# M_prev's products on quarters of TensorE's array, attention ordered anew, and a second quarter of weights split early

## The chip, the core and the metric

The kernel runs on one NeuronCore of a Trainium2 chip. The core has five engines, each with its own queue that it works through in order: PE (TensorE, the matmuls; PEld is its weight load), DVE (VectorE), ACT (ScalarE), POOL (GpSimd) and SP (SyncE, which here only issues transfers). The metric is the device time of one execution in microseconds (us). Before the change the median of 3 runs is 961.65 us (960.67 to 963.48).

## The reference

Three stages follow each other. Each one's output is the next one's input.

```python
# attention, with B, H, S, D = 4, 8, 576, 64
scores = q @ k.T / sqrt(D), causal;  a = softmax(scores);  local = a @ v
q_p = where(q > 0, q, exp(q) - 1) + 1
mem_out = (q_p @ M_prev) / (q_p @ z_prev + 1e-6)
x = g * mem_out + (1 - g) * local          # g = sigmoid(beta), one number per head
# mixture of experts: 2304 tokens, 8 experts, 512 -> 1024 -> 512
logits = x @ w_gate;  e = argmax(logits);  p = softmax(logits)[e]
x = p * (relu(x @ w1[e]) @ w2[e])
# last network: 512 -> 2048 -> 512
out = elu(x @ w_in) @ w_out
```

All arrays are float32.

## The kernel before, in words

Attention works on 16 pairs of heads (`pair(p)`), four pairs to a batch. For one pair, in the names of the code: q and k are loaded and transposed on PE (L568); `parts` makes a high and a low part of each in `ab` (L582 or L585, then L589); `phi_in` and the two steps behind it make q_p in `qpT`, the exponential and the positive part on ACT (L602 to L610), the rest on POOL (L626, L627); `scores` makes five blocks of query rows (L665 and L669 for blocks 0 to 3, L676 and L677 for block 4), DVE takes each block's extreme (L685), ACT the exponential `a` (L690); `weights` transposes `a` on PE (L703) and ACT or DVE copies it out to `aA` and `aB` (L515, L518); L804 multiplies with v, giving `xT`. Two products on quarters of the array follow (helper `quarters`, L527): `mb` with `qpT` for the memory, and `iw` with `xT` for the logits. DVE scales them into `ms` and `ls` (L781 to L789, L824) and POOL adds them up (L836). All of these products share four PSUM buffers of two banks (`pat`).

Ahead of the first pair, `constants` loads M_prev into `mb`, transposes its 32 matrices on PE (L340), copies them out (L344) and multiplies each with `w_gate` (L353), so that `mb` holds M_prev, M_prev times w_gate, and z_prev (L354). Matmuls without a use (`keep_busy`, L249) run meanwhile.

After every fourth pair `gate_plan` finds each token's expert and rank on DVE and PE (L871 to L950), after the third batch `routing` decides what the first four tiles of 128 tokens are, SP loads the first tile's weights (L1167), and POOL gathers the first tile's rows (L1181, into the buffer `ex` that `phi_in` used last). `first_parts` splits these rows (L1192) and the first of the eight quarters of the tile's weights (L1209 or L1206 for the high part, L1212 for the low) while attention still runs. The second stage, `moe`, then takes the tiles (L1335 and L1378 are its products, three for each in high and low parts), and at the same time widens the last network's weights through the buffers `wide` (class `Widen`); `moe2` is the last stage.

What sets the order: every step is an `Op` of a planner (`Plan`) with its engines, a cost number, what it reads and writes, and a priority. `order` simulates the engines with the cost numbers, picks at each step the ready operation with the lowest priority number on an engine that is free, and the program is emitted in that order, engine by engine. Of two engines it takes the one that would end first. `stick` keeps PE in one shape of the array as long as something of that shape is ready. The priorities' offsets are the table `KNOBS`. Nothing is reordered on the chip: an engine waits for the instruction at the head of its queue.

Of the kernel before, what the change touches and what calls it, by code (L numbers as in the profile page):

```python
# [24 lines left out]
NI = 5  # L25
# [58 lines left out]
class Plan:  # L84
# [52 lines left out]
    def order(self):  # L137
# [7 lines left out]
        while len(done) < len(self.ops):  # L145
# [43 lines left out]
            if e == "PE":  # L189

                n = int(t / self.TICK)
                cold = work.get(n - 1, self.warm if n == 0 else 0.0) < self.DUTY * self.TICK
                end = t + o.cost * (1.0 + cold) + (self.wait if o.waits else 0.0) + (self.DRAIN if o.mode != mode else 0.0)
                mode = o.mode
                for m in range(n, int(end / self.TICK) + 1):
                    part = min(end, (m + 1) * self.TICK) - max(t, m * self.TICK)
                    work[m] = work.get(m, 0.0) + o.dense * o.cost * part / max(1.0, end - t)
# [56 lines left out]
def constants(tc, ctx, c, M_prev, z_prev, beta, w_gate):  # L254
# [78 lines left out]
    for h in range(2):  # L333
        for n in range(2):
            def mk(h, n):
                bk = Slot(c.rs)

                def f():
                    for x in range(8):
                        nc.tensor.transpose(bk.t[0:D, x * D:(x + 1) * D], c.mb[hss[h], 8 * n + x, 0:D], c.ident[hss[h], hss[h]])  # L340
                pl.op("PE", 450, f, r=["mld"], w=[bk], prio=K["mem"] - 30)

                def f():
                    nc.scalar.copy(mT[:, h, 8 * n:8 * n + 8, :].rearrange("p x d -> p (x d)"), bk.t[0:D, 0:512])  # L344
                pl.op("ACT", ca(512), f, r=[bk], w=[("mT", h, n)], prio=K["mem"] - 30)
            mk(h, n)
    for h in range(2):
        def mk(h):
            bq = Slot(c.rs)

            def f():
                for x in range(NPAIR):
                    nc.tensor.matmul(bq.t[hss[h], x * E:(x + 1) * E], mT[:, h, x, :], wg[:, 2 * (x % (H // 2)) + h, :], start=True, stop=True)  # L353
                nc.tensor.matmul(bq.t[hss[h], 256:256 + B * H], zr, c.ident[0:B * H, 0:B * H], start=True, stop=True)  # L354
            pl.op("PE", 900, f, r=["mld", ("mT", h, 0), ("mT", h, 1), ("raw", 0, 0), ("raw", 0, 1)], w=[bq], prio=K["mem"] - 20, dense=0.15)

            def f():
                nc.vector.tensor_copy(c.mb[hss[h], :, D:XB], bq.t[hss[h], 0:NPAIR * E].rearrange("p (x e) -> p x e", e=E))
                nc.vector.tensor_copy(c.mb[hss[h], :, XB:MW].rearrange("p x o -> p (x o)"),
                                      bq.t[hss[h], 256:256 + B * H].rearrange("p (x h) -> p x h", h=2)[:, :, h])  # L360
            pl.op("DVE", 400, f, r=[bq], w=["mb"], prio=K["mem"] - 20)
        mk(h)
# [100 lines left out]
def cps(n):  # L463
    return 330 + 0.83 * n


def cpt(n):
    return 150 + 2.1 * n


def attention(tc, ctx, c, q, k, v, M_prev):
# [19 lines left out]
    r_q, r_k = padded("q", K["nq"], [P, NI, 2, D], lambda t: t[0:D, NI - 1]), padded("k", K["nq"], [P, NI, 2, D], lambda t: t[D:P, NI - 1])  # L491
# [369 lines left out]
def gate_plan(tc, c, b, lg, xrow, rl, rx, ring, pr):  # L861
# [4 lines left out]
    def bc(x):  # L866
# [4 lines left out]
        (330, lambda: v.tensor_reduce(G.L, lg.t.rearrange("p i c e -> p i e c"), axis=AX.X, op=ALU.add)),  # L871
# [772 lines left out]
def kernel(ctx, tc, q, k, v, M_prev, z_prev, beta, w_gate, w1, w2, w_in, w_out, out):  # L1644
# [41 lines left out]
    with ExitStack() as s1:  # L1686
# [3 lines left out]
        c.wq = [[ep.tile([P, 1024], F32R, name=f"wq{n}{i}") for i in range(2)] for n in range(1)]  # L1690
# [82 lines left out]
```

## Time and profile before

| | |
|---|---|
| median of 3 runs | 961.65 us |
| the profiled execution | 961.42 us, of which the span from the first to the last instruction is 959.7 us |
| attention, to the first product of the first tile | 0 to 245.5 us |
| mixture of experts, to the last network's first product | 245.5 to about 553 us |
| last network | about 553 us to the end |
| PE busy | 930.1 us, 97% of the span |
| DVE, ACT, POOL busy | 639.3, 447.4, 181.5 us |

The profile records one execution. A row of a timeline gives the start, the duration from the first instruction of the row to the end of its last, the engine, the code's line, output and inputs, and how many instructions were merged; in brackets stands how long the engine sat idle before, and what ended it. A float32 product that isn't a transpose shows as two records. PEclk is the clock that TensorE was granted, 1.00 for 2.4 GHz and 0.50 for 1.2 GHz; a stretch in which it changes shows a value between.

### The profile page before, as it was taken

The page shows a single profiled execution, that of the slowest core. Times are in us where ns is not written, and L with a number is a line of the kernel's source. Part 1 is how long each engine was busy: PE and PEld are TensorE (multiplying, and loading weights), DVE is VectorE, ACT ScalarE, POOL GpSimd, SP SyncE. Part 2 cuts the span into 40 slices and gives each one's busy share as a digit, 9 for nine tenths or more (in the row PEclk, how much of TensorE's full clock was granted, in tenths as well). Part 3 has the DMA queues.
Part 4 walks back from the last instruction along what each step waited for, and adds up shares of the span by engine and source line. Part 5 has one row for each costly group of instructions (what it writes and reads, how often), then busy time and mean ns, then how long its engine had stood idle before and what let it go on. Part 6 is the DMA issues. An engine that isn't in the chain of part 4 may idle for free. (4 is left out here: it accounts for less than half of the span.)

```text
span 959.7 us, 18446 instructions
## 1 busy us (share of the span) xinstructions
PE 930.1 (97%) x6858; PEld 771.6 (80%) x6858; DVE 639.3 (67%) x1179; ACT 447.4 (47%) x902; POOL 181.5 (19%) x244
## 2 busy tenths in 40 slices
PE   9998999999899999999999999999999999999996
PEld 6777878877678888888888789988888888888895
DVE  4888878877775568646898596555565556555553
ACT  4777768767464347536876562221122121212221
POOL 3443442433300122222221100010001000100000
PEclk8999999979999999999999999999999999999999
DMA  6323334253542697569997370110011000100000
GB/s 123 88 65 100 76 76 111 53 174 103 208 132 87 227 340 250 169 222 361 326 339 281 120 236 1 34 44 1 1 44 45 1 14 21 44 0 1 12 34 23
DMA packets 96596, 110.00 MB, mean 115 GB/s; under 512 B 64878, under 2 KB 64878, under 8 KB 94192
## 3 DMA queue, kind: packets, MB, share of 16 engines
q1 hardware_dynamic: 90496, 95.25, 31.6%
q0 software_dynamic: 4800, 13.18, 3.9%
q8 instruction: 55, 0.90, 0.4%
q10 hardware_dynamic: 1200, 0.30, 0.2%
q14 instruction: 45, 0.37, 0.1%
HBM read 87.94 MB, written 23.41 MB: 116 GB/s over the span
## 5 line engine op out<-in xcount | busy, mean ns | idle before, releaser
L1586 ACT ACTIVATE elu<-pt 128x512 f32<-128x512 f32 x72 | 43.2, 600 | 268.7 <-PE pt L1578 266.6
L1611 PE MATMUL pt<-w,gh 128*128 128x512 f32 x432 | 134.4, 392 | 0.5 <-DVE gh L1490 0.5
L1378 PE MATMUL pm<-w,hh 128*128 128x512 f32 x368 | 126.2, 404 | 0.8 <-ACT y L1391 0.8
L1594 DVE TENSOR_SCALAR elu<-elu 128x512 f32<-128x512 f32 x72 | 30.7, 427 | 129.8 <-ACT elu L1586 129.8
L1611 PEld LDWEIGHTS pt<-w,gh 128*128 128x128 f32 x432 | 79.5, 188 | 17.1 <-DVE gh L1490 0.9
L690 ACT ACTIVATE a<-pat,st 128x128 f32<-128x128 f32 (+2 forms) x144 | 78.1, 551 | 22.5 <-DVE st L685 21.4
L1611 PE MATMUL pt<-w,gl 128*128 128x512 f32 x216 | 84.4, 391 | 0.0
L1378 PEld LDWEIGHTS pm<-w,hh 128*128 128x128 f32 x368 | 69.2, 188 | 16.1 <-ACT y L1391 1.2
L1378 PE MATMUL pm<-w,hl 128*128 128x512 f32 x184 | 73.2, 398 | 0.3 <-DVE hl L1212 0.3
L685 DVE TENSOR_REDUCE st<-pat 128x2 f32<-128x256 f32 (+4 forms) x80 | 63.8, 807 | 9.3 <-PE pat L669 9.3
L1578 PE MATMUL pt<-yTh,w 128*128 128x256 f32 (+1 forms) x288 | 68.8, 319 | 0.0
L703 PE MATMUL pat<-ident,a 128*128 128x128 f32 x400 | 57.9, 290 | 8.6 <-ACT a L690 8.3
L626 POOL TENSOR_SCALAR ex<-ex 128x512 f32<-128x512 f32 (+1 forms) x32 | 37.9, 1185 | 133.0 <-ACT ex L602 133.0
L703 PEld LDWEIGHTS pat<-ident,a 128*128 128x128 f32 x400 | 45.4, 147 | 16.1 <-ACT a L690 15.2
L1598 DVE SCALAR_TENSOR_TENSOR tnh<-tnh,elu 128x512 f32<-128x512 f32 x72 | 49.7, 691 | 7.7 <-ACT tnh L1590 1.7
L1335 PE MATMUL pm<-w,x 128*128 128x512 f32 x216 | 51.9, 392 | 1.3 <-DVE w L1212 0.9
L1493 DVE TENSOR_TENSOR gl<-tnh,gh 128x512 fp32r<-128x512 f32 x72 | 49.6, 691 | 4.2
L1578 PEld LDWEIGHTS pt<-yTh,w 128*128 128x128 f32 x288 | 48.6, 189 | 4.5
L1602 DVE SCALAR_TENSOR_TENSOR tnh<-pt,tnh 128x512 f32<-128x512 f32 x72 | 49.6, 691 | 3.3
L1335 PEld LDWEIGHTS pm<-w,x 128*128 128x128 f32 x216 | 40.2, 188 | 10.4 <-DVE w L1212 1.4
L1212 DVE TENSOR_TENSOR hl<-pm,hh 128x512 fp32r<-128x512 f32 x46 | 31.4, 685 | 25.3 <-ACTq L1309 14.8
L1611 PEld LDWEIGHTS pt<-w,gl 128*128 128x128 f32 x216 | 40.5, 188 | 9.2 <-DVE gl L1493 0.4
(342 smaller groups left out, 2115.5 us busy)
## 6 DMA issues: line engine op xcount, KB each, us to landing
wraw<-in_moe_w_dram SPq DMA_DIRECT2D x24, 1024.0 KB
wrbw<-in_moe_w_dram SPq DMA_DIRECT2D x12, 1024.0 KB
wide<-in_moe_w_in_dram SPq DMA_DIRECT2D x16, 512.0 KB
wf<-half SPq DMA_DIRECT2D x32, 256.0 KB
wide<-in_moe_w_out_dram SPq DMA_DIRECT2D x16, 512.0 KB
wide<-wf SPq DMA_DIRECT2D x9, 512.0 KB
q<-in_q_dram SPq DMA_DIRECT2D x32, 128.0 KB
v<-in_v_dram SPq DMA_DIRECT2D x32, 128.0 KB
```

What stands on the lines that cost most here:

```text
L626: nc.gpsimd.tensor_scalar(e, e, 1.0, 0.0, op0=ALU.min, op1=ALU.add)
L685: nc.vector.tensor_reduce(ss.t[:, 2 * i:2 * i + (2 if i < 4 else 1)], src(), axis=AX.X if i < 4 else AX.XY, op=ALU.min)
L690: nc.scalar.activation(sa[i].t[:, h, :] if i < 4 else sa[4].t[:, 0:S].rearrange("p (y n) -> p y n", y=2), src()[:, h, :] if i < 4 else src ...
L703: nc.tensor.transpose(w.t[:, y:y + P], t[:, j * P:(j + 1) * P], c.ident)
L1335: nc.tensor.matmul(g[hf].t, a.t[:, cc, :], b[:, 512 * hf:512 * (hf + 1)], start=(cc == 0 and n == 0), stop=(cc == 3 and n == 2))
L1378: nc.tensor.matmul(y.t, a.t[:, 2 * (q % 2) + jj, :], b[:, 512 * jj:512 * (jj + 1)], start=(q == 0 and jj == 0 and n == 0), stop=(q == 3 an ...
L1493: nc.vector.tensor_sub(lo(), src(), hi().bitcast(F32))
L1578: nc.tensor.matmul(h.t[:, n * j + n0:n * j + n1], w(cc, a, ft), b(cc), start=(cc == 0 and x == 0), stop=(cc == 3 and x == 2))
L1586: nc.scalar.activation(se.t, h.t, AF.Exp)
L1598: nc.vector.scalar_tensor_tensor(st.t, st.t, 0.0, se.t, op0=ALU.min, op1=ALU.mult)
L1602: nc.vector.scalar_tensor_tensor(st.t, h.t, 0.0, st.t, op0=ALU.max, op1=ALU.add)
L1611: nc.tensor.matmul(acc[a].t, y.t[:, n * j + P * a:n * j + P * (a + 1)], wsub(1, k, ft // 2)[:, ft % 2, :], start=(ft == 0 and x == 0), sto ...
```

## The change

M_prev's matrices lie in two halves of the partitions. Before, each is transposed by PE's transpose into the lower 64 partitions, one after the other, and multiplied there. Now the transpose is a product with the identity that stays in its own half, so that the two halves alternate between two quarters of the array (new lines L341, L353, L355). `w_gate` is loaded twice for that, once for each half. The planner is told that its second stretch of time begins slow, the cost numbers of four operations are set anew (two of POOL's, DVE's reduction in `gate_plan`, the new products), and the offsets of attention are others; of these the diff shows two lines. q's buffers lie in `wide` instead of ones of their own, and the room goes to a second pair `wq`, so that `first_parts` also splits the second quarter of the first tile's weights.

```diff
-                cold = work.get(n - 1, self.warm if n == 0 else 0.0) < self.DUTY * self.TICK
+                cold = (n == 1 and self.warm < self.TICK) or work.get(n - 1, self.warm if n == 0 else 0.0) < self.DUTY * self.TICK
...
-    "m_g": -500, "wq": 0.64, "sa": 60.0, "sm": 50.0, "s2": 0.0, "step": -68438.62, "hd": -241.62,
-    "mem": 379947.52, "xg": 4,
+    "m_g": -500, "wq": 0.64, "sa": 60.0, "sm": 50.0, "s2": 0.0, "step": -71105.58, "hd": 10338.26,
+    "mem": 164377.47, "xg": 4,
...
-    wg = c.wraw[0][1][0:D, 0:H * E].rearrange("d (h e) -> d h e", e=E)
+    wg = c.wraw[0][1][:, 0:H * E].rearrange("d (h e) -> d h e", e=E)
...
-    mT = c.wraw[0][0][0:D, :].rearrange("p (h x d) -> p h x d", h=2, x=NPAIR)
+    mT = c.wraw[0][0][:, 0:NPAIR * D].rearrange("p (x d) -> p x d", x=NPAIR)
...
             nc.sync.dma_start(c.mb[hss[h], :, 0:D], Mv[h])
-        nc.sync.dma_start(wg, w_gate.rearrange("(h d) e -> d h e", d=D))
+            nc.sync.dma_start(wg[hss[h]], w_gate.rearrange("(h d) e -> d h e", d=D))
...
-                        nc.tensor.transpose(bk.t[0:D, x * D:(x + 1) * D], c.mb[hss[h], 8 * n + x, 0:D], c.ident[hss[h], hss[h]])
+                for x in range(8):
+                    for h in range(2):
+                        nc.tensor.matmul(bk.t[hss[h], 512 * h + x * D:512 * h + (x + 1) * D], c.mb[hss[h], 8 * n + x, 0:D], c.ident[hss[h], hss[h]], start=True, stop=True)
...
-                    nc.tensor.matmul(bq.t[hss[h], x * E:(x + 1) * E], mT[:, h, x, :], wg[:, 2 * (x % (H // 2)) + h, :], start=True, stop=True)
+        for x in range(NPAIR):
+            for h in range(2):
+                nc.tensor.matmul(bq.t[hss[h], 512 * h + x * E:512 * h + (x + 1) * E], mT[hss[h], x, :], wg[hss[h], 2 * (x % (H // 2)) + h, :], start=True, stop=True)
...
-    return 330 + 0.83 * n
+    return 240 + 3.3 * n
...
-    return 150 + 2.1 * n
+    return 150 + 2.2 * n
...
-    r_q, r_k = padded("q", K["nq"], [P, NI, 2, D], lambda t: t[0:D, NI - 1]), padded("k", K["nq"], [P, NI, 2, D], lambda t: t[D:P, NI - 1])
+
+    r_q = Ring("q", [t[:, 0:NI * 2 * D].rearrange("p (i h d) -> p i h d", i=NI, h=2) for t in c.wide])
...
-        (330, lambda: v.tensor_reduce(G.L, lg.t.rearrange("p i c e -> p i e c"), axis=AX.X, op=ALU.add)),
+        (700, lambda: v.tensor_reduce(G.L, lg.t.rearrange("p i c e -> p i e c"), axis=AX.X, op=ALU.add)),
...
-        c.wq = [[ep.tile([P, 1024], F32R, name=f"wq{n}{i}") for i in range(2)] for n in range(1)]
+        c.wq = [[ep.tile([P, 1024], F32R, name=f"wq{n}{i}") for i in range(2)] for n in range(2)]
```

Five lines more stand in the changed file from `attention` on, so that L568 is now L573, L527 is L532, L804 is L809 and L1335 is L1340.

On PE at the start of the program, from the last matmul without a use to the first scores, before (`pat` are the PSUM buffers, `wraw` holds the transposed matrices and w_gate):

```order
L340 MATMUL pat_93<-ident,mb 64x64 x8
L340 MATMUL pat_91<-ident,mb 64x64 x8
L340 MATMUL pat_94<-ident,mb 64x64 x8
L340 MATMUL pat_92<-ident,mb 64x64 x8
L568 MATMUL pat_93<-ident,k_195 128x128 x5
L353 MATMUL pat_91<-wraw_74,wraw_73 64x8 x16
L354 MATMUL pat_91<-ident,wraw_74 64x32
L568 MATMUL pat_94<-ident,q_191 128x128 x5
L353 MATMUL pat_92<-wraw_74,wraw_73 64x8 x16
L354 MATMUL pat_92<-ident,wraw_74 64x32
L249 LDWEIGHTS identb
```

and now, in the same place:

```order
L341 MATMUL pat_95<-ident,mb 64x64 x16
L341 MATMUL pat_93<-ident,mb 64x64 x16
L249 LDWEIGHTS identb
L249 MATMUL pat_94<-ones,identb 128x512
L249 LDWEIGHTS identb
L249 MATMUL pat_96<-ones,identb 128x512
L573 MATMUL pat_94<-ident,k_195 128x128 x5
L249 LDWEIGHTS identb
L249 MATMUL pat_95<-ones,identb 128x512
L249 LDWEIGHTS identb
L249 MATMUL pat_96<-ones,identb 128x512
L353 MATMUL pat_95<-wraw_74,wraw_73 64x8 x32
```

Behind these come L355 and q's transposes, then three matmuls without a use and the scores; before, four of them stood behind the second L354. All products of M_prev are now ahead of q's transposes, in one run.

On PE in the middle of attention, from a pair's last transposes of `a` to the next pair's scores, before (`q_191` is a load of q, `aA_224` and `aB_226` are a pair's transposed weights, `ab_199` the next pair's parts):

```order
L748 MATMUL pat_91<-st_221,swap 128x1
L568 MATMUL pat_93<-ident,q_191 128x128 x5
L527 MATMUL pat_92<-mb,qpT_229 64x73 x20
L527 MATMUL pat_91<-iw,xT_231 64x72 x20
L804 MATMUL pat_94<-aA_224,v_205 64x384 x2
L804 MATMUL pat_94<-aA_224,v_205 64x256 x2
L804 MATMUL pat_94<-aA_224,v_205 64x128 x2
L804 MATMUL pat_92<-aB_226,v_205 64x192 x8
L804 MATMUL pat_92<-aB_226,v_205 64x64 x2
L665 MATMUL pat_91<-ab_199 128x256 x6
```

and now, first the same place, then the place behind the four first blocks of scores:

```order
L753 MATMUL pat_93<-st_219,swap 128x1
L573 MATMUL pat_95<-ident,wide_70 128x128 x5
L809 MATMUL pat_96<-aA_223,v_203 64x384 x2
L809 MATMUL pat_96<-aA_223,v_203 64x256 x2
L809 MATMUL pat_96<-aA_223,v_203 64x128 x2
L809 MATMUL pat_94<-aB_225,v_203 64x192 x8
L809 MATMUL pat_94<-aB_225,v_203 64x64 x2
L670 MATMUL pat_93<-ab_200 128x256 x6
```

```order
L674 MATMUL pat_94<-mask_112,id_113 128x64
L532 MATMUL pat_93<-mb,qpT_229 64x73 x20
L532 MATMUL pat_96<-iw,xT_231 64x72 x20
L681 MATMUL pat_95<-ab_200 128x288 x6
```

The two products on quarters have moved from ahead of the multiplication with v to behind the scores' fourth block, and the memory's product is now that of the pair whose q was transposed just before; it used to come one pair later.

On DVE at the place where the first tile's weights are split, before (`wq_82` is the high part, `wq_83` the low):

```order
L685 TENSOR_REDUCE st_219<-pat_94 128x2
L1209 CAST wq_82<-wraw_73 128x1024
L685 TENSOR_REDUCE st_219<-pat_93 128x1
L1212 TENSOR_TENSOR wq_83<-wraw_73,wq_82 128x1024
L950 TENSOR_TENSOR r_tab<-r_tab,pat_91 72x256
```

and now:

```order
L761 SCALAR_TENSOR_TENSOR st_221<-st_221,omg 128x10
L1214 CAST wq_82<-wraw_73 128x1024
L1214 CAST wq_84<-wraw_73 128x1024
L1217 TENSOR_TENSOR wq_83<-wraw_73,wq_82 128x1024
L1217 TENSOR_TENSOR wq_85<-wraw_73,wq_84 128x1024
L765 RECIPROCAL st_221<-st_221 128x10
L594 SCALAR_TENSOR_TENSOR ab_199<-pat_93,ab_199 128x640
```

Four operations on 1024 columns now stand in one run, ahead of the low part of q (`ab_199`) that the next pair's scores read.

## Rows read from the trace of the kernel before

**Rows 1.** The page: each engine's busy time, its share of the span, its instructions.

```profile
PE 930.1 (97%) x6858; PEld 771.6 (80%) x6858; DVE 639.3 (67%) x1179; ACT 447.4 (47%) x902; POOL 181.5 (19%) x244
```

**Rows 2.** Busy time by stretch: PE, PEld, DVE, ACT, POOL; then PEclk, DMA share, GB/s.

```profile
62.30:245.50 183.20, 172.01 (x2626) 142.54 (x2624) 145.99 (x341) 133.44 (x364) 74.15 (x88) 0.96 0.35 94
285.00:543.00 258.00, 256.02 (x1233) 211.55 (x1232) 181.34 (x253) 148.09 (x215) 52.09 (x56) 1.00 0.71 245
```

**Rows 3.** The same view, two stretches of 20 us in which the clock fell.

```profile
0.00:20.00 20.00, 18.11 (x153) 12.56 (x153) 5.95 (x19) 6.68 (x14) 7.91 (x34) 0.83 0.76 132
200.00:220.00 20.00, 18.30 (x213) 14.88 (x213) 15.19 (x56) 12.82 (x39) 5.87 (x7) 0.74 0.70 256
```

**Rows 4.** The same view, the microsecond before the fall after 200 us.

```profile
203.00:204.00 1.00, 0.30 (x6) 0.18 (x4) 1.00 (x2) 1.00 (x4) 0.00 (x0) 1.00 0.70 262
```

**Rows 5.** The timeline of the start: start, us, engine, line, operation, [idle before].

```profile
2.33 0.94 SPq L307 DMA_DIRECT2D wraw<-in_moe_w_gate_dram  x1
...
6.84 1.78 PE L340 MATMUL pat<-ident,mb 64*64 64x64 f32 x32
7.51 2.03 ACT L344 COPY wraw<-pat 64x512 f32<-64x512 f32 x4 [3.64 <-PE pat L340]
...
9.25 2.03 PE L353 MATMUL pat<-wraw,wraw 64*64 64x8 f32 x32
...
12.13 2.99 PE L353 MATMUL pat<-wraw,wraw 64*64 64x8 f32 x32
...
17.21 1.01 PE L665 MATMUL pat<-ab 64*128 64x256 f32 x6
...
28.32 0.86 PE L527 MATMUL pat<-mb,qpT 64*64 64x73 f32 x40
```

**Rows 6.** PE's timeline over two pairs, the second with a gate in it.

```profile
62.34 0.41 PE L703 MATMUL pat<-ident,a 128*128 128x128 f32 x2
...
75.35 0.41 PE L703 MATMUL pat<-ident,a 128*128 128x128 f32 x2
...
88.15 1.06 PE L676 MATMUL pat<-ab 128*128 128x288 f32 x6 [0.67 <-ACT a L690]
...
90.54 0.66 PE L703 MATMUL pat<-ident,a 128*128 128x128 f32 x4 [0.81 <-ACT a L690]
```

**Rows 7.** DVE's timeline in the pair with the gate.

```profile
85.91 0.79 DVE L871 TENSOR_REDUCE gL<-raw 128x40 f32<-128x320 f32 x1 [0.85 <-POOL raw L836]
```

**Rows 8.** The timeline of the last pairs: q's transposes, POOL's work on q, v's product, scores.

```profile
225.54 0.74 PE L568 MATMUL pat<-ident,q 128*128 128x128 f32 x5
...
226.51 0.71 ACT L602 ACTIVATE ex<-pat 128x640 f32<-128x640 f32 x1
...
227.30 1.92 POOL L626 TENSOR_SCALAR ex<-ex 128x512 f32<-128x512 f32 x1 [9.01 <-ACT ex L602]
...
227.63 1.51 PE L804 MATMUL pat<-aA,v 128*64 128x384 f32 x12
...
230.49 0.62 PE L665 MATMUL pat<-ab 64*128 64x256 f32 x6
...
231.36 2.02 POOL L836 TENSOR_TENSOR raw<-ms,ls 128x80 f32<-128x80 f32 x3
...
233.26 0.83 PEld L676 LDWEIGHTS pat<-ab 128*128 128x128 f32 x6
```

**Rows 9.** DVE's timeline at the split of the first quarter of weights.

```profile
221.15 0.69 DVE L1209 CAST wq<-wraw 128x1024 fp32r<-128x1024 f32 x1
...
222.42 1.22 DVE L1212 TENSOR_TENSOR wq<-wraw,wq 128x1024 fp32r<-128x1024 f32 x1
```

**Rows 10.** PE's timeline from the gathered rows to the first tile's products.

```profile
237.30 0.72 PE L1192 MATMUL pat<-ident,ex 128*128 128x128 f32 x4 [1.21 <-DMA ex<-xd,r_tok]
...
247.46 0.70 PE L1335 MATMUL pm<-w,x 128*128 128x512 f32 x2 [0.31 <-DVE w L1209]
249.11 3.92 PE L1335 MATMUL pm<-w,x 128*128 128x512 f32 x16 [0.94 <-DVE w L1212]
```

More of the change, by code (lines that the diff above doesn't have):

```diff
@@ L226 @@
     "m_lag": 0.0, "m_if": 700.0, "m_fl": -3000.0, "m_wl": 300.0, "wa": 0, "wa0": 10022.449169040721, "wa1": 23927.854833523612, "wt": 1, "wp": 16, "wj": 2000.0,
-    "m_g": -500, "wq": 0.64, "sa": 60.0, "sm": 50.0, "s2": 0.0, "step": -68438.62, "hd": -241.62,
-    "mem": 379947.52, "xg": 4,
+    "m_g": -500, "wq": 0.64, "sa": 60.0, "sm": 50.0, "s2": 0.0, "step": -71105.58, "hd": 10338.26,
+    "mem": 164377.47, "xg": 4,
     "wh": [("ACT", "DVE"), ("ACT", "DVE"), ("ACT", "DVE"), ("DVE",), ("ACT",), ("ACT", "DVE"), ("ACT", "DVE"), ("ACT", "DVE")],
     "wl": [("DVE",)] * 8, "ord": [3, 4, 2, 1, 0], "rings": 4, "ab": 2, "nq": 2, "nv": 2, "na": 2, "na4": 2, "nx": 2, "nls": 2, "wide": 1, "de": ("DVE", "POOL"),
-    "busy": [0, 0, 0], "early": -20000.00, "late": 500, "mld": -243107.35, "gate": -11056.04,
+    "busy": [0, 0, 0], "early": -20000.00, "late": 500, "mld": -245742.92, "gate": -77771.75,
     "warm": [52, 0.0, 200.0], "qe": ("POOL",),
-    "off": {"dg": -456858.19, "tk": -15281.37, "tq": 326102.56, "hi": 227591.46, "lo": 685795.94, "px": -804771.37, "phi": -821561.11, "F": -5913.349368048794, "S": -226778.90, "min": 700452.14, "exp": 141498.79, "T": 171120.25, "Te": 329591.10, "fin": 220855.96, "mm": -44823.69, "md": 277870.24, "ms": 762170.63, "av": 103888.21, "ave": 159075.03, "rw": 352456.97, "ls": 191517.20, "add": -155361.26},
-    "wait": 25, "first": 18775.53, "stick": 733899.31
+    "off": {"dg": -605835.61, "tk": 15401.64, "tq": 324169.31, "hi": 405818.35, "lo": 1055487.07, "px": -598125.62, "phi": -346862.51, "F": -5913.349368048794, "S": -90140.54, "min": -457.02, "exp": 74328.86, "T": 182753.96, "Te": 148916.14, "fin": 292827.46, "mm": -280376.83, "md": 539146.97, "ms": 657086.07, "av": -50881.99, "ave": 195966.06, "rw": 298047.87, "ls": 84750.20, "add": 292692.78},
+    "wait": 25, "first": 23028.25, "stick": 645649.79
 }
@@ L332, in constants @@
     pl.op("DVE", 200, f, w=["g"], prio=K["mem"])
[L333 to L339, printed above, removed]
-                        nc.tensor.transpose(bk.t[0:D, x * D:(x + 1) * D], c.mb[hss[h], 8 * n + x, 0:D], c.ident[hss[h], hss[h]])
[L341 to L346, printed above, removed]
@@ L347, in constants, with mk, f @@
-    for h in range(2):
-        def mk(h):
-            bq = Slot(c.rs)
-            def f():
-                for x in range(NPAIR):
-                    nc.tensor.matmul(bq.t[hss[h], x * E:(x + 1) * E], mT[:, h, x, :], wg[:, 2 * (x % (H // 2)) + h, :], start=True, stop=True)
[L354 to L362, printed above, removed]
+    for n in range(2):
+        def mk(n):
+            bk = Slot(c.rs)
+            def f():
+                for x in range(8):
+                    for h in range(2):
+                        nc.tensor.matmul(bk.t[hss[h], 512 * h + x * D:512 * h + (x + 1) * D], c.mb[hss[h], 8 * n + x, 0:D], c.ident[hss[h], hss[h]], start=True, stop=True)
+            pl.op("PE", 450, f, r=["mld"], w=[bk], prio=K["mem"] - 30, mode=3)
+            for h in range(2):
+                def f(h=h):
+                    nc.scalar.copy(mT[hss[h], 8 * n:8 * n + 8, :].rearrange("p x d -> p (x d)"), bk.t[hss[h], 512 * h:512 * (h + 1)])
+                pl.op("ACT", ca(512), f, r=[bk], w=[("mT", n, h)], prio=K["mem"] - 30)
+        mk(n)
@@ new lines, in constants, with f @@
+    bq = Slot(c.rs)
+    def f():
+        for x in range(NPAIR):
+            for h in range(2):
+                nc.tensor.matmul(bq.t[hss[h], 512 * h + x * E:512 * h + (x + 1) * E], mT[hss[h], x, :], wg[hss[h], 2 * (x % (H // 2)) + h, :], start=True, stop=True)
+        for h in range(2):
+            nc.tensor.matmul(bq.t[hss[h], 512 * h + 256:512 * h + 256 + B * H], zr, c.ident[0:B * H, 0:B * H], start=True, stop=True)
+    pl.op("PE", 1200, f, r=["mld", ("raw", 0, 0), ("raw", 0, 1)] + [("mT", n, h) for n in range(2) for h in range(2)], w=[bq], prio=K["mem"] - 20, dense=0.5, mode=3)
@@ L363, in constants, with f @@
+    def f():
+        for h in range(2):
+            nc.vector.tensor_copy(c.mb[hss[h], :, D:XB], bq.t[hss[h], 512 * h:512 * h + NPAIR * E].rearrange("p (x e) -> p x e", e=E))
+            nc.vector.tensor_copy(c.mb[hss[h], :, XB:MW].rearrange("p x o -> p (x o)"),
+                                  bq.t[hss[h], 512 * h + 256:512 * h + 256 + B * H].rearrange("p (x h) -> p x h", h=2)[:, :, h])
+    pl.op("DVE", 800, f, r=[bq], w=["mb"], prio=K["mem"] - 20)
     routing_constants(tc, c)
@@ L488, in tail @@
         return t[D:P, NI - 1, :, :]
-    r_q, r_k = padded("q", K["nq"], [P, NI, 2, D], lambda t: t[0:D, NI - 1]), padded("k", K["nq"], [P, NI, 2, D], lambda t: t[D:P, NI - 1])
+    r_q = Ring("q", [t[:, 0:NI * 2 * D].rearrange("p (i h d) -> p i h d", i=NI, h=2) for t in c.wide])
+    for t in r_q.tiles:
+        nc.gpsimd.memset(t[0:D, NI - 1], 0.0)
+    r_k = padded("k", K["nq"], [P, NI, 2, D], lambda t: t[D:P, NI - 1])
     r_ab = sb("ab", K["ab"], [P, 4 * QW + 2 * P], F32R)
```

## The prediction

> **What bounds the kernel now.** I read the page's busy times first: PE is at work in 97% of the span, so only PE's idle time, PE's slow time and PE's own work can move the end [rows 1]. The table by stretch then says where there is any. From 285 to 543 us PE idles 2.0 us of 258 at full clock; the tuned part behind attention gives nothing back and takes nothing, so what the first 285 us win or lose arrives whole at the end [rows 2]. In attention proper (62.3 to 245.5 us) PE idles 11.2 of 183.2 us, and the granted clock is 0.96: (1 - 0.96) x 183.2 / 0.5 = 14.7 us at the lower of its two levels, 1.2 GHz. Work that PE does at that level takes twice its time, so these stretches cost up to 7.3 us [rows 2]. Of them 10.4 us lie behind 200 us, and the first 20 us hold 6.8 us more [rows 3]. The timelines come last, for who waits there.
>
> A plain pair takes 75.35 - 62.34 = 13.01 us, and PE is not idle for more than tenths in it. A pair with a gate loses more: block 4's scores wait 0.67 us and the transposes 0.81 us, both for ACT's exponentials [rows 6]. The cause is on DVE, where the gate's reduction of 0.79 us sits in front of the four reductions that the exponentials need [rows 7]. In the third gate PE is busy 0.30 of the microsecond after 203 us, and the clock is low right behind it [rows 3, 4].
>
> **The start.** Before, from the end of the transposes (6.84 + 1.78 = 8.62 us) to the first scores at 17.21 PE is never free: it is PE's queue that makes the scores late [rows 5]. Now the transposes are 32 float32 products, two records each. The only quarters in the trace do 40 records in 0.86 us [rows 5], on four quarters. Two quarters at that rate each need 64 x 0.86 / 40 = 1.4 us if two do as much as four, 2.8 us if half; I take 1.9, near the 1.78 of before, so they end at 8.8. M_prev's second half now lands behind the first w_gate load, many small packets; no row prices that, PE's queue of L249 covers some, and I add 0.5 us (0 to 1). Two of the four copies (2.03 us for four [rows 5]) follow the last transposes: 10.4. The products, again 64 records, took 2.03 and 2.99 us in two runs of 32, the second while the clock fell [rows 5]. On two quarters: 1.4 us by the four-quarter rate, 4.1 if nothing overlaps (2 x 2.03); I take 2.0, half of that: 12.4. L355 and q's transposes (0.74 [rows 8], with some 0.3) bring 13.5, and the high and low part of q some 1.6 more (the same 0.7 and 0.8 as the operations on 640 columns [rows 8]): scores at 15.1, 2.1 us earlier. Of the 6.8 us at the lower clock [rows 3] the part that the first scores lie in may go, as the products are shorter: I add 0.5. The start gives **2.6 us** (bounds: 5.0, with the low clock gone, and a loss of 0.5, with no overlap and M_prev 1 us late).
>
> One rule speaks against this part: the Trainium skill, TensorEngine Tiling (Array Packing), Performance Considerations, says that each matmul has some 60 cycles of overhead and that no tiling factor should be taken from a dimension that is small already. The products here move 8 columns. By that rule they would stay near 4.1 us, and the start would give 0.5 us in place of 2.6. The trace leans the other way: 73 columns on quarters cost 0.86 / 40 = 22 ns a record, 8 columns on one quarter 2.03 / 32 = 63 ns [rows 5], so what the quarters share is not the columns alone; 8 columns on two quarters no row here shows.
>
> **Attention's order.** The work on PE is the same, and so is the number of changes between shapes of the array in a pair, four. What changes is who is waited for. The memory's product now stands 0.67 (q's transposes, up to the next operation) + 2.86 (v, 227.63 to 230.49) + 2.77 (four blocks of scores, to 233.26) = 6.3 us behind the start of q's transposes. It needs `qpT`, which is done 231.36 - 225.54 = 5.8 us behind it [rows 8]. Until now a whole pair lay between the two. So 0.5 us are left, and for a plain pair I take no change: its small waits may go (0.4 us a pair) or turn into waits for POOL (0.5 us if ACT begins 1 us later). Over some ten plain pairs that is -4 to +5 us; I take +0.5.
>
> With gates the order should help: the reduction `gL`, whose cost number was half of what it takes, now stands behind the four blocks' reductions, so the 0.67 and 0.81 us of waits [rows 6] should go, three times: 4.4 us. Against it, the table product of the gate (L948) now comes right behind v's product, about 4 us behind the rank product, while DVE has some twenty small operations and a low part between them; before, it came most of a pair later. No row prices that wait; it lies between 0 and the 1.5 us that it replaces, and I take 0.9, three times: 2.7. Net gain 1.7 us. The low clock of 14.7 us (7.3 us of cost) begins after such waits [rows 4]; with shorter ones part of it should stay away, but a single short gap is enough, and new gaps come. I take a third back, **2.4 us** (bounds 0 and 7.3, or a loss of 3 if one more fall comes). Attention's order so gives 1.7 + 2.4 - 0.5 = **3.6 us**.
>
> **The weights' second quarter.** DVE now does 2 x 0.69 + 2 x 1.22 = 3.8 us in one run [rows 9] ahead of q's low part (0.8 us), which the next scores need. PE covers this with q's transposes, v's product and the logits' product, 0.67 + 2.86 + some 0.7 = 4.2 us [rows 8]. DVE starts about with q's transposes, so the scores come at 3.8 + 0.2 + 0.8 + 0.1 = 4.9 us: a wait of 0.7, with what it does to the clock and to the four reductions behind it a loss of **1.0 us** (0 to 3.8). If the transfer of the weights weren't there in time, this run would hold up all of DVE; I expect it to land some 2 us ahead.
>
> What it buys is at the first tile. PE waits 0.31 and 0.94 us there for the second quarter's parts [rows 10]; the third quarter's low part then is late by some 0.35 us in turn: a gain of **0.9 us** (0.3 to 1.3). The gathered rows, which PE awaits 1.21 us [rows 10], are fetched by POOL behind 2.02 us of sums [rows 8]; now these sums stand ahead of POOL's last work on q, and the fetch comes right behind that. I take **1.0** of 1.21.
>
> **The sum.** The profiled execution took 961.42 us, 1.7 more than its span, and lies 0.2 under the median. 961.4 - 2.6 - 3.6 + 1.0 - 0.9 - 1.0 = 954.3; I forecast 954.5 us.
>
> **Rivals.** (a) The gates and the clock give nothing, since the table's waits replace the old ones and the falls come again elsewhere. For it: the falls so far follow gaps of under a microsecond [rows 4], which no planner aims at. Against it: `gL` does leave the reductions' way. Then 3.6 becomes -0.5, and the time is about 958.5; with a start by the skill's rule 960.6. (b) Slower: the memory's product waits for POOL in every pair. The place is L532 behind the fourth block; the point from which it decides is an exponential on ACT that begins over 0.5 us later than in the rows, because the copies of `aB` are ahead of it in ACT's queue. At 1.5 us later the wait is 1.0 us, in 15 pairs 15 us; the transposes' small waits, 0.2 us a pair, go in exchange: 954.5 + 15 - 3 = 966.5. For it: the margin is 0.5 us out of 5.8, and the planner puts an operation where it is just ready. Against it: POOL's cost number, which was under half of the 1.92 us measured [rows 8], is now right, so the planner sees the wait coming, and DVE takes more of the copies. (c) The start doesn't gain, since k and q of the next pairs land as before and the early lead is spent waiting for them: 954.5 + 2.6 + 1, about 958.
>
> **How the numbers follow.** Forecast 0.60, its own range 950 to 957.5; (a) 0.18; (c) 0.08; (b) 0.14. A measurement here tells 0.3%, 2.9 us, from no change: faster means under 958.8, slower over 964.5. Faster: 0.60, half of (a) and a third of (c), 0.72; slower: (b) but for the sixth of it with waits so short that the time stays under the bound, 0.12; same: the rest, 0.16. The range reaches over (a) and (c) toward (b), and below to the start and the clock both at their best: 948 to 963.
>
> **What would show it.** In the profile of the changed kernel: first scores near 15 us; no 0.7 us wait of L681 in a gate's pair, but one of L948 for DVE; L532 with waits for POOL under 0.2 us; the low clock in fewer than 14.7 us of attention; scores of one of the last pairs waiting some 0.7 us behind L1217; L1340 without a wait for the second quarter. I am wrong if the plain pair is longer than 13.0 us, if the first scores come after 16.5 us, or if the time is over 960.

## The result, and the profile after

The changed kernel takes 965.97 us (median of 14 runs, 963.2 to 973.01) against 960.67 us of the kernel before (14 runs): the ratio is 1.0065, 95% interval 1.0049 to 1.008. It is slower by 0.65%, where 954.5 us was forecast. The execution profiled took 970.05 us, 4.1 us above the median.

The page's busy times of the changed kernel, as [rows 1] of before:

```profile
PE 931.9 (96%) x6893; PEld 772.4 (80%) x6893; DVE 656.1 (68%) x1189; ACT 439.8 (45%) x892; POOL 183.0 (19%) x244
```

PE's busy time is what it was, within 2 us. Its share fell by one point because it stands idle longer. A table by stage of the changed kernel tells where (us, PE busy (instructions), then PEld, DVE, ACT, POOL, clock, DMA share, GB/s): attention, the first tiles with the late gate (the last batch's, which is worked in beside the first tiles), the tiles up to the last network, and its start.

```profile
62.59:246.99 184.40, 169.15 (x2549) 140.75 (x2549) 160.47 (x346) 129.32 (x356) 76.22 (x88) 0.99 0.37 99
246.99:285.00 38.01, 34.55 (x176) 27.24 (x177) 27.19 (x77) 16.48 (x26) 6.48 (x8) 0.91 0.52 172
285.00:549.61 264.61, 260.59 (x1255) 215.06 (x1253) 184.35 (x257) 150.10 (x218) 52.49 (x56) 1.00 0.69 239
```

In attention PE idles 15.25 us (11.2 before [rows 2]), at nearly full clock: of the two low stretches [rows 3], 200 to 220 us is at 1.00 now. From 247 to 285 us it idles 3.5 us (3.1 before), and at a mean clock of 0.91 it spends (1 - 0.91) / 0.5 = 18% of the stretch, nearly 7 us, at the lower level, 1.2 GHz; before, this stretch had full clock. From 285 us to the last network it idles 4.0 us, twice as much as [rows 2].

How far each kernel is ahead of the kernel before at one and the same piece of work shows it more closely. The table is worked out from the starts of rows on PE's timelines, before's among them (minus: ahead; e1 to e10 are the experiments below). Each column is one profiled execution, and e9's, at 961.88 us, was the slowest of its ten (median 957.52):

| us ahead (-) or behind (+) at | changed | e6 | e1 | e5 | e8 | e9 | e4 | e3 | e10 |
|---|---|---|---|---|---|---|---|---|---|
| first scores (17.21) | -1.8 | -2.1 | -1.9 | -1.7 | -1.7 | -2.0 | -2.0 | -1.5 | 0.0 |
| v's product, second pair (42.77) | -1.4 | -3.4 | -3.0 | -1.3 | -3.3 | -3.1 | +0.9 | -0.7 | -0.1 |
| same, ninth pair (137.01) | +2.2 | +0.6 | -1.2 | +0.9 | -1.1 | -0.3 | +1.0 | -0.7 | -0.2 |
| first tile's first product (245.50) | +1.5 | -1.4 | -7.1 | -3.4 | -7.3 | -4.1 | -3.9 | -1.9 | +0.2 |
| first tile's second layer (254.62) | -0.1 | -3.0 | -8.7 | -4.7 | -6.9 | -5.2 | -3.9 | -3.5 | -1.4 |
| transposes of a tile's rows in `ex` (290.22) | +6.3 | +3.5 | +2.9 | +1.9 | -6.9 | -6.1 | -3.9 | +0.5 | +4.2 |
| last network's first product (542.36) | +7.3 | +5.0 | +2.4 | +2.1 | -4.3 | -0.5 | -2.9 | +0.4 | +3.0 |
| last product's end (951.41) | +8.6 | +4.6 | +1.9 | +1.6 | -2.8 | +0.5 | -3.0 | +1.4 | +3.0 |

The last network's first product (L1578) begins at 542.36 us in the kernel before, not at the "about 553" of the table of times before.

**The start.** PE's timeline of the changed kernel (start us, us, engine, line, operation, tiles, shapes, count, [idle before <- releaser]):

```profile
7.55 2.54 PE L341 MATMUL pat<-ident,mb 64*64 64x64 f32 x64
...
11.54 2.03 PE L353 MATMUL pat<-wraw,wraw 64*64 64x8 f32 x64
...
15.43 1.30 PE L670 MATMUL pat<-ab 64*128 64x256 f32 x6
...
22.03 0.85 PE L708 MATMUL pat<-ident,a 128*128 128x128 f32 x6
...
40.48 0.28 PE L753 MATMUL pat<-st,swap 128*128 128x1 f32 x2
...
53.83 0.28 PE L753 MATMUL pat<-st,swap 128*128 128x1 f32 x2
```

The last two rows (L753) stand at the end of two plain pairs. Against [rows 5] the products (now L353 x64) took 2.03 us in one run instead of 2.03 and 2.99 in two, and the first scores stand at 15.43 instead of 17.21. But the clock was 0.87 in the first 20 us, the scores ran at half rate where before they no longer did, and the first transposes of `a` (L708) begin at 22.03, as before. e6, whose program is the same up to the tiles, had clock 1.00 there and begins them at 19.49.

**The first tile.** PE, as [rows 10]:

```profile
239.59 0.60 PE L1197 MATMUL pat<-ident,ex 128*128 128x128 f32 x3 [0.63 <-DMA ex<-xd,r_tok]
...
246.99 3.02 PE L1340 MATMUL pm<-wq,x 128*128 128x512 f32 x12 [0.68 <-DVE ls L829]
...
249.85 3.35 PE L1340 MATMUL pm<-w,x 128*128 128x512 f32 x12
```

The wait for the gathered rows is 0.63 us for 1.21, and the two waits for the second quarter's parts are gone.

**A gate.** First PE, then DVE, then POOL at the first gate of the changed kernel:

```profile
82.25 1.52 PE L809 MATMUL pat<-aA,v 128*64 128x384 f32 x12
...
85.11 0.25 PE L948 MATMUL pat<-raw,qone 128*72 128x128 bf16 x1
87.34 1.22 PE L948 MATMUL pat<-raw,qone 128*72 128x128 bf16 x19 [1.99 <-DVE raw L941]
...
92.86 1.06 PE L681 MATMUL pat<-ab 128*128 128x288 f32 x6
...
94.80 0.66 PE L708 MATMUL pat<-ident,a 128*128 128x128 f32 x4 [0.58 <-DVE ms L794]
```

```profile
83.18 0.71 DVE L926 TENSOR_SCALAR raw<-col,grq 128x128 bf16<-128x128 f32 x1
83.82 0.28 DVE L929 TENSOR_SCALAR qone<-col,grq 128x144 bf16<-128x144 f32 x1
...
84.62 0.63 DVE L929 TENSOR_SCALAR qone<-col,grq 128x144 bf16<-128x144 f32 x1
...
85.25 1.35 DVE L929 TENSOR_SCALAR qone<-col,grq 128x144 bf16<-128x144 f32 x1
...
86.92 0.37 DVE L941 TENSOR_SCALAR raw<-raw,row 128x640 bf16<-128x640 bf16 x1
```

```profile
83.21 1.95 POOL L631 TENSOR_SCALAR ex<-ex 128x512 f32<-128x512 f32 x1 [4.44 <-ACT ex L607]
85.24 1.26 POOL L632 TENSOR_TENSOR qpT<-ex,qpT 128x512 f32<-128x512 f32 x1
```

The old waits of 0.67 and 0.81 us for ACT's exponentials [rows 6] are gone from this pair, as forecast, but the transposes L708 now wait 0.58 us for DVE's `ms`, and L948, the table product, waits 1.99 us for `raw`. `gL` [rows 7] was done early (at 77.40 us). What is late is the ten small one-hot operations (L926, L929; those left out took 0.16 to 0.28 us each): three of them, beside POOL's work on q, took 0.71, 0.63 and 1.35. The long one begins with POOL's L632 and ends 0.1 us behind it. The second and third gate read the same (L948 waits 1.99 and 1.58 us). In the kernel before, these operations ran where POOL had none:

```profile
96.40 0.28 DVE L924 TENSOR_SCALAR qone<-col,grq 128x144 bf16<-128x144 f32 x1
96.61 0.38 DVE L936 TENSOR_SCALAR raw<-raw,row 128x640 bf16<-128x640 bf16 x1
...
96.82 1.94 POOL L626 TENSOR_SCALAR ex<-ex 128x512 f32<-128x512 f32 x1 [9.29 <-ACT ex L602]
```

**The late gate.** DVE, then PE, then two windows of the changed kernel:

```profile
270.25 0.15 DVE L915 TENSOR_TENSOR gsli<-gsl,inval 128x5 uint32<-128x5 f32 x1
270.42 2.36 DVE L1321 TENSOR_TENSOR wq<-wraw,wq 128x1024 fp32r<-128x1024 f32 x2
272.69 0.16 DVE L916 TENSOR_SCALAR gsli<-gsli 128x5 uint32<-128x5 uint32 x1
272.77 2.35 DVE L1321 TENSOR_TENSOR w<-wraw,w 128x1024 fp32r<-128x1024 f32 x2
...
277.45 0.38 DVE L941 TENSOR_SCALAR raw<-raw,row 128x640 bf16<-128x640 bf16 x1
```

```profile
276.13 0.22 PE L948 MATMUL pm<-raw,qone 128*72 128x128 bf16 x1 [0.96 <-DVE raw L926]
277.89 2.18 PE L948 MATMUL pm<-raw,qone 128*72 128x128 bf16 x19 [1.54 <-DVE raw L941]
```

```profile
276.00:280.00 4.00, 2.33 (x20) 2.16 (x21) 3.53 (x17) 1.31 (x5) 0.00 (x0) 0.69 0.00 0
280.00:284.00 4.00, 4.00 (x18) 3.35 (x18) 1.26 (x7) 0.00 (x0) 0.91 (x1) 0.50 0.00 0
```

Two runs of L1321, the low parts of the third tile's weights, 2.36 and 2.35 us, stand between the gate's steps of 0.2 us; L948 waits 0.96 and 1.54 us behind them, and the clock falls for nearly 7 us. Before, the same four low parts (L1316) were done ahead of the gate's first step here, L907, and PE waited once, 1.18 us. DVE, then PE, of the kernel before:

```profile
265.38 1.23 DVE L1316 TENSOR_TENSOR wq<-wraw,wq 128x1024 fp32r<-128x1024 f32 x1 [0.25 <-ACT wq L1311]
266.52 3.49 DVE L1316 TENSOR_TENSOR w<-wraw,w 128x1024 fp32r<-128x1024 f32 x3
...
270.76 0.20 DVE L907 TENSOR_TENSOR geq<-pm,ebase 128x40 f32<-128x40 f32 x1
```

```profile
271.31 0.16 PE L1005 MATMUL pm<-r_act,triu 72*72 72x1 bf16 x1 [1.18 <-DVE r_act L996]
```

Counted from the first tile's first product, the low parts now come 3.6 us later (23.4 for 19.9) and the gate's first step 2.7 us earlier (22.5 for 25.3).

### The profile page after: what moved, and what is told of

Same layout as the page of the kernel before. It is cut to its first block, busy times and chain, and to the rows that moved or that the text cites. A ratio compares the mean times of both kernels' runs of the same rounds, so it can differ in the third digit from the quotient of the medians.

```text
span 968.3 us, 18473 instructions
## 1 busy us (share of the span) xinstructions
PE 931.9 (96%) x6893; PEld 772.4 (80%) x6893; DVE 656.1 (68%) x1189; ACT 439.8 (45%) x892; POOL 183.0 (19%) x244
## 5 line engine op out<-in xcount | busy, mean ns | idle before, releaser
L690 DVE TENSOR_REDUCE st<-pat 128x2 f32<-128x256 f32 (+4 forms) x80 | 60.8, 804 | 2.7 <-PE pat L674 2.3
L708 PE MATMUL pat<-ident,a 128*128 128x128 f32 x400 | 53.4, 278 | 1.8 <-DVE ms L794 1.8
L708 PEld LDWEIGHTS pat<-ident,a 128*128 128x128 f32 x400 | 43.5, 141 | 5.9 <-ACT a L695 2.7
L670 PE MATMUL pat<-ab 64*128 64x256 f32 (+2 forms) x384 | 47.0, 364 | 0.7 <-DVE ab L594 0.4
L1350 ACT ACTIVATE h<-pm 128x512 f32<-128x512 f32 x44 | 25.9, 597 | 45.9 <-PE pm L1340 44.4
```

The costliest lines, as they stand in the source:

```text
L670: nc.tensor.matmul(s.t[:, 512 * h:512 * h + m], row(y)[hs, i * P:(i + 1) * P], row(x)[hs, 0:m], start=(k == 0), stop=False)
L690: nc.vector.tensor_reduce(ss.t[:, 2 * i:2 * i + (2 if i < 4 else 1)], src(), axis=AX.X if i < 4 else AX.XY, op=ALU.min)
L708: nc.tensor.transpose(w.t[:, y:y + P], t[:, j * P:(j + 1) * P], c.ident)
```

## The experiments

Theory P says that POOL's work on q holds DVE's one-hot operations up at the three gates. Rival G: the product stands too early whatever POOL does. Theory L: the second quarter leads the planner to put the third tile's low parts among the late gate's steps. Rival S: the loss is in the code, not in the order. "Before" took 960.3 to 961.0 us beside each of the runs.

**e1, POOL's work left out in three pairs.** The features of q are unfinished there, and with them the tokens' experts and what the tiles load. Of the changed line only the argument that differs is shown.

```diff
- [{"DVE": fv, "POOL": fp}[x] for x in es]
+ [{"DVE": fv, "POOL": (lambda: None) if p in (5, 9, 13) else fp}[x] for x in es]
```

> The changed kernel, with POOL's four operations on q (the minimum and the sum that finish qpT) left out in the three pairs that follow a gate's last pair; the order on PE, DVE and ACT stays. Theory P (POOL's work on q stretches DVE's one-hot operations, 0.28 us each alone, to 0.63 and 1.35 us, some 1.9 us a gate): the table product L948 waits under 0.3 us at each of the three gates instead of 1.99, 1.99 and 1.58; no one-hot operation is over 0.35 us; 5.5 us of waits and up to 1.8 us of low clock go, so 958.5 to 961 us. Rival G (the product simply stands too early, DVE's chain is too long): the waits stay at 1.5 us or more and the time at 965 to 967 us.

963.46 us, ratio 1.0031 (1.0016 to 1.0046). PE's rows of L948 at the three gates:

```profile
83.90 1.22 PE L948 MATMUL pat<-raw,qone 128*72 128x128 bf16 x19 [0.26 <-DVE raw L941]
...
139.23 1.22 PE L948 MATMUL pat<-raw,qone 128*72 128x128 bf16 x19 [0.32 <-DVE raw L941]
...
194.83 1.22 PE L948 MATMUL pat<-raw,qone 128*72 128x128 bf16 x19
```

The waits are 0.26, 0.32 and none: P, not G. At the first tile the kernel is 7.1 us ahead, 5.7 us more than e6 at the same clock; 4.7 of these lie in the three pairs with L948 (from one L809 to the next). The time fell less, since with other experts the second tile reads and splits weights that the change skips (a run of L1321 at 248.79 us), and from 245 to 290 us 10 us are lost; the total can't be read as P's price.

**e2, the order alone**: before with the change's table of numbers and costs (diff as in the change).

> The kernel before with the table of numbers and the costs of the change alone: M_prev's products as before, one quarter of the weights split early, q in its own buffers. Theory P: the loss is in the order, at the gates and at the late gate; it comes without the rest of the change, 965 to 969 us. Rival S (the loss is in the code: the second quarter's run on DVE, q in the widening's buffers): 958 to 962 us.

961.08 us, 1.0018 (1.0001 to 1.0036). This lies in rival S's range. L943 (L948 of the change) waits 5.6 us in three gates here too, so P's waits come with the order; but the late gate is as before (one wait of 1.18 us), and alone the order loses under 1 us by the medians.

**e3, the code alone**, with before's numbers and costs, and **e4, M_prev's quarters alone**.

> The changed kernel with the table of numbers and the costs of before: M_prev's products on quarters, the second quarter split early and q in the widening's buffers stay. Theory P: faster than before by the start's 1.4 us and about 1.5 us at the first tile, less 1 us for DVE's run: 957.5 to 960.5 us. Rival S: 964 us or more.

> The kernel before with M_prev's products on quarters alone. If the start's lead lasts through attention: first scores near 15.4 us, 1.4 us gained, 959.3 us. If it is spent by the low clock and waits: within 0.5 us of before, 960.7 us. If the new start disturbs the order behind it: over 962.5 us.

e3: 962.76 us, 1.0026 (1.0012 to 1.0039). e4: 958.54 us, 0.9985 (0.997 to 1.0). e3 lies between its two ranges. The quarters alone give 1.8 us, which e4's interval bounds by 0 and 2.9. Its profile doesn't show where: the lead of 2.0 us at the first scores is gone by the second pair, and the 3.9 us at the first tile come with a clock of 1.00 from 200 to 220 us, where before's profile had 0.74. e3's loss then points to the second quarter, which e10 tests. e3's L948 waits in the late gate exactly as the changed kernel's (0.96, 1.54), e4's doesn't.

**e5, the same work done by DVE** in those three pairs, everything else in its place.

```diff
- [{"DVE": fv, "POOL": fp}[x] for x in es]
+ [{"DVE": fv, "POOL": fv if p in (5, 9, 13) else fp}[x] for x in es]
```

> The changed kernel; in the three pairs that follow a gate's last pair the minimum and the sum on q's features (two of the 16 steps a pair) are done by DVE in one operation each instead of by POOL; nothing else moves. Theory P (POOL's operations block DVE's one-hot operations): the 1.9 us of stretch a gate goes, DVE has 0.7 us more ahead of the last one-hot operations; L948 waits 0.6 to 1.0 us a gate instead of 1.9, and the time is 2.5 to 4 us under the changed kernel's 965.97: 962 to 963.5 us. Rival G (DVE's chain is simply too long for the place): DVE has more to do, the waits rise to 2.5 us, 967 us or more.

961.78 us, 1.0009 (0.9997 to 1.0021): 4.2 us under the changed kernel. DVE at the first gate:

```profile
83.49 0.28 DVE L926 TENSOR_SCALAR raw<-col,grq 128x128 bf16<-128x128 f32 x1
83.69 0.68 DVE L627 SCALAR_TENSOR_TENSOR qpT<-ex,qpT 128x512 f32<-128x512 f32 x1
84.29 0.29 DVE L929 TENSOR_SCALAR qone<-col,grq 128x144 bf16<-128x144 f32 x1
...
85.69 0.38 DVE L941 TENSOR_SCALAR raw<-raw,row 128x640 bf16<-128x640 bf16 x1
```

All ten one-hot operations of this gate take 0.28 or 0.29; L948 waits 0.86, 0.93 and 0.54 us. DVE has more to do and PE waits less: P is shown, and G's rise to 2.5 us didn't come. What is left of the waits (2.3 us, 0.6 in e1) is DVE's own chain. In the three pairs with L948 e5 is 2.7 us faster than e6; the rest of the 4.2 isn't placed.

**e6, the late gate's due time 500 smaller; e7, e5 and e6 together.**

```diff
- "busy": [0, 0, 0], "early": -20000.00, "late": 500,
+ "busy": [0, 0, 0], "early": -20000.00, "late": 0,
```

> The changed kernel with one number, the due time of the late gate (the last batch's, worked in beside the first tiles), 500 smaller, so that DVE does the gate's small operations ahead of the low parts of the third tile's weights. Theory L (two such runs of 2.35 us, planned at 0.7, hold the gate's table product up; it costs 2.5 us of wait and up to 3.4 us of low clock, against 1.2 us of wait before the change): L948's 0.96 and 1.54 us of wait go, clock 1.00 from 265 to 290 us, and 2.5 to 6 us of time: 960 to 963.5 us. Rival: PE then waits for the weights' low parts in exchange, no gain, 965 to 967 us.

> The changed kernel with the edits of e5 and e6 together. Theories P and L together, with places that don't touch: the gains add, 956.5 to 960.5 us, no slower than the kernel before. If one loss hides behind the other: 962 us or more.

967.51 us, 1.007 (1.0056 to 1.0085), and 963.67 us, 1.0029 (1.0017 to 1.0042): no gain, but 1.5 us more than the changed kernel and 1.9 more than e5. The two runs of L1321 had only moved from in front of L941 to in front of L1033, and the wait with them:

```profile
270.55 1.22 PE L948 MATMUL pm<-raw,qone 128*72 128x128 bf16 x19 [0.84 <-DVE r_off L1021]
...
275.70 0.37 PE L1039 MATMUL pm<-r_sel,ev 72*1 72x21 f32 x4 [3.18 <-DVE r_sel L1033]
```

**e9, the late gate whole ahead of them** (e5 with "late" at -1000).

> e5's kernel with the late gate's due time 1500 smaller than in the change, so that all its operations on DVE, L1033's and the table's sum among them, stand ahead of the low parts of the third tile's weights; in e6 the two products behind them had only changed places (L948 waited 0.9 us, L1039 3.2). Theory L: L948 and L1039 wait under 0.5 us in sum, the clock is 1.00 from 265 to 290 us; against e5 a gain of 2 to 4 us: 958 to 960 us. Rival (DVE's two runs of 2.35 us must be paid in this stretch wherever they stand, since the first tiles are bound by DVE): waits of the same sum appear at the tiles' own products, 961 to 964 us.

957.52 us, 0.9963 (0.995 to 0.9975): 4.3 us under e5, 8.5 under the changed kernel, and under the kernel before. PE and DVE in the late gate:

```profile
259.69 1.28 PE L948 MATMUL pm<-raw,qone 128*72 128x128 bf16 x20
```

```profile
264.09 2.36 DVE L1321 TENSOR_TENSOR wq<-wraw,wq 128x1024 fp32r<-128x1024 f32 x2 [0.44 <-ACT wq L1316]
266.52 2.35 DVE L1321 TENSOR_TENSOR w<-wraw,w 128x1024 fp32r<-128x1024 f32 x2
```

And its busy time from 265 to 290 us:

```profile
265.00:290.00 25.00, 25.00 (x123) 20.77 (x122) 17.84 (x25) 13.54 (x21) 3.23 (x2) 1.00 0.43 134
```

Neither L948 nor what follows waits; PE is busy all of these 25 us. The same two runs, now behind the gate's steps, hold nothing up here: L is shown, and the rival's waits at the tiles' own products don't appear in this stretch. In this profile, the slowest of the ten executions, the lead of 6.1 us at 290 us is spent by the end, 5.6 of it ahead of the last network (L1365 waits 3.06 us for ACT near 501 us). By the medians 4.3 us stay.

**e10, the second quarter alone; e11, q in the widening's buffers alone.**

> The kernel before with the second quarter split early and q in the widening's buffers alone (M_prev and the table of numbers as before). Theory L: the late gate loses as in e3 (waits of 2.5 us at L948, where before there was 1.2 us), and the first tile gains 1.6 us: 961.5 to 965 us. Rival (e3's loss comes from the quarters' start going together with it): 959 to 961 us.

> The kernel before with q in the widening's buffers alone. The buffers are free while q is used, so no theory has a price for it: 960 to 961 us, no wait of over 1 us that the kernel before doesn't have. If q's place delays a load or the first widening, over 962 us.

e10: 963.2 us, 1.0024 (1.0012 to 1.0035); L948's waits (here L946) of 0.98 and 1.54 are there, the first tile gains 1.6 us, the late gate loses 5.6. e11: 960.95 us, 1.0006 (0.999 to 1.0022): the buffers cost nothing that can be measured.

The parts don't add up to the whole. Alone, by the medians, the quarters give 1.8 us, the order costs 0.8 and the second quarter with q's buffers 2.5: 1.6 us together, where the change costs 5.3. No run assigns the other 3.7 us; e5 and e9 show only that mending the two waits brings back 8.5.

**e8, the change without the second quarter**, with e5's edit.

```diff
-        c.wq = [[ep.tile([P, 1024], F32R, name=f"wq{n}{i}") for i in range(2)] for n in range(2)]
+        c.wq = [[ep.tile([P, 1024], F32R, name=f"wq{n}{i}") for i in range(2)] for n in range(1)]
```

q's ring is that of before as well.

> The changed kernel without its second quarter split early and with q in its own buffers (as before), and with e5's edit. Theory L says that the second quarter moves the low parts of the third tile's weights into the late gate: without it no wait at L948 in the late gate; theory P: L948's waits at the three gates under 1.0 us each. Quarters -1.75 us, order with its gates mended -3 us or more, against before: 954 to 957.5 us, faster than both kernels. Rival: the order itself loses, 960 us or more.

958.03 us, 0.9956 (0.9938 to 0.9973), faster than both kernels, but 6.9 us ahead at 290 us and 2.8 at the end. PE idles near 500 us, behind ACT:

```profile
499.01 0.66 PE L1362 MATMUL pm<-ident,h 128*128 128x128 f32 x4 [2.82 <-ACT h L1347]
```

```profile
497.81 0.66 ACT L1127 ACTIVATE half<-wide 128x512 f32<-128x512 f32 x1 [4.97 <-DMA wide<-in_moe_w_in_dram]
498.38 1.07 ACT L1347 ACTIVATE h<-pm 128x512 f32<-128x512 f32 x2
```

ACT waits for a read of the widening (L1127, L1130 in the change), and the tile's `h` is queued behind it.

**e12, the widening's parts earlier (0.60 for 0.64); e13 and e14, e9 and e8 with such a read planned at 2200 for 1456**, so that ACT takes it behind `h`.

> e8's kernel with the widening's parts spread over tiles at 0.60 of a tile each instead of 0.64. Theory B: e8 reaches the middle of the tiles 6.9 us ahead of the kernel before and ends 2.8 us ahead, because ACT waits 5.0 us for a transfer of the second layer's weights (L1127) with the tile's copy of h behind it, and the last rows' transfer waits too; with the parts issued earlier PE's 2.8 us of wait at L1362 goes: 954.5 to 956.5 us. Rival (the transfers are as fast as the memory gives them, earlier ones only push the tiles' own weights back): 957.5 us or more.

> e9's kernel with the planned time of a widening's read (512 KB) raised from 1456 to 2200, so that ACT's operation on it (L1130) is planned behind the tile's copies of h instead of ahead of them. Theory B (the lead of e8 and e9, 6 to 7 us in the middle of the tiles, is given back near 500 us by one wait of ACT for such a read, with h queued behind it): PE's 3 us of wait at L1365 goes, and with it 2 to 4 us: 953.5 to 956 us. Rival (the transfers bound that stretch, whoever waits for them): the wait moves to the next layer's weights, 957 us or more.

> e8's kernel with the same number. Theory B: 2.8 us of wait at L1362 goes, 954.5 to 956.5 us. Rival: 957.5 us or more.

959.96, 980.5 and 980.19 us: no gain in e12 (e8 took 958.03), and a loss of over 20 us in e13 and e14 against e9 and e8. In e13 the wait for `h` went (in e14 one of 2.90 us is left), but the last parts came after the tiles:

```profile
541.42 2.93 PE L1583 MATMUL pt<-raw1n,raw0n 128*128 128x256 f32 x12 [6.42 <-ACTq L1738]
...
568.68 1.11 PE L1551 MATMUL pt<-ident,wraw 128*128 128x128 f32 x4 [15.33 <-DMA wraw<-yd]
```

In these runs the widening has no slack, earlier or later. What sets it isn't settled.

## Why the prediction was wrong

**The start**: sized rightly in the main. The products took 2.03 us, forecast as 2.0. The transposes took 2.54 us in the changed kernel's profile for 1.9, and M_prev's transfer held them up by 0.3 to 1.7 us where runs show a wait (0.5 taken). First scores came at 15.43 for 15.1. What this lead is worth at the end is less sure: e4 gains 1.8 us (0 to 2.9) of the 2.6. In the profiles of e4 and of the changed kernel the lead is spent by 22 us, by the lower clock and not by rival (c)'s loads; in e6's it isn't.

**Attention's order**: here the prediction failed first, at the step on the table product, "No row prices that wait; it lies between 0 and the 1.5 us that it replaces, and I take 0.9". It was 1.99, 1.99 and 1.58 us: 5.6 us for 2.7. The bound was taken from the wait that goes, though the move put DVE's one-hot operations beside POOL's work on q, which [rows 8] showed to be busy just behind q's transposes. Nothing in the trace of before had the two at one time, so what it shows of either alone was no bound.

Two smaller terms were too good. The old waits of 4.4 us at the gates went, but the transposes wait 0.6 us for `ms` in each of the three pairs in their place (1.8 us), which the sum has at nothing. Plain pairs take 13.06 to 13.35 us (53.83 - 40.48), over the 13.0 that I had set as a bound; in ten pairs block 4's scores wait 0.27 us for ACT.

The low clock of the third gate [rows 3, 4] did go, but that may be luck: from 200 to 220 us it was 1.00 in e4 and 0.91 in e11 as well, which keep the order of before. "A single short gap is enough" isn't borne out either: e6 has the three waits of 1.6 to 2.0 us and a clock of 1.00 from 62 to 245 us.

Without the overlap (e1) attention is 7.1 us ahead, and the prediction's terms up to there, 2.6 + 3.6 - 1.0 + 1.0, make 6.2. That they agree may be luck in part, since e1 leaves POOL's work out altogether and its profile had full clock from the start. Rival (a) named the cause, the table's waits, and priced it too low; (b) didn't come: POOL's end holds L532 in no pair.

**The weights' second quarter**: the parts that were priced came near: in e10 DVE's run costs 1.2 us at the fifteenth pair (1.0 taken), of which 0.4 are left at the sixteenth, and the first tile gains 1.6 us (0.9); in the changed kernel the gathered rows gave 0.6 us of the 1.0 taken. The step that failed is "What it buys is at the first tile": what it costs behind that tile wasn't asked, and stood in the sum at nothing. With the second quarter done early the third tile's low parts no longer stand ahead of the late gate's steps but among them, and each pair takes 2.36 us. That cost 5.6 us in e10 and 6.4 in the changed kernel. The planner counts 0.7 us for such a pair, one number for tiles that reuse their expert's weights and skip it and for those that don't; that this number led to the place is likely, but no run changed it.

**The end**: "what the first 285 us win or lose arrives whole at the end" is wrong as well: e8 keeps 2.8 of 6.9 us.

The sum: with both waits mended (e9) the time is 957.52 us, 3.0 over the 954.5 forecast. That is a gain of 3.2 us on the kernel before beside it, where 7.1 were forecast, so more than these two waits was missing; the 8.5 us between e9 and the changed kernel are what the two edits give.

## What to carry to other kernels

When an order moves, ask of each moved operation who else works at its new place: a duration measured beside an idle engine is no bound beside a busy one. Look up where a planned cost is one number for taken and skipped branches, and what stands behind the taken one. A mended wait should be checked by where the time goes next: in e6 it had only changed its product.

## What the runs showed of the hardware

A DVE operation of 0.28 us (float32 in, bfloat16 out, 128x144) took 1.35 us when it began together with POOL's sum of two 128x512 tiles (1.26 us), in all three gates; beside POOL's minimum (1.95 us) two of six or seven took 0.63 to 0.71 and the rest some 0.28. The Trainium skill, SBUF — State Buffer, "Who interferes with whom", says that VectorE in its two-port modes and GpSimd contend for a shared pair of ports and that the second to issue is blocked fully until the first is done. For the sum the trace agrees (DVE ends 0.1 us behind POOL); beside the minimum most operations pass at full rate, which full blocking would not allow. In which mode these operations run, no trace here shows.

64 records of float32 products of 8 columns take 2.03 us on two quarters of the array at a time; on one, 32 took 2.03 at best [rows 5], so they overlap nearly whole. The Trainium skill, TensorEngine Tiling (Array Packing), Performance Considerations, gives each matmul some 60 cycles of overhead and advises against a tiling factor from a dimension that is small already; whether two quarters pay this overhead at one time it doesn't say there. The 4.1 us in the prediction were a reading of that rule, and the trace doesn't bear it out for this shape.
